# Grouped-query attention on one core: K transposed on VectorE in 32x32 blocks, scores in 32-row PE tiles, Q loaded plainly and replicated

## The chip, the cores and the metric

The kernel runs on one core of a Trainium2 chip. The metric is the device time of one execution in microseconds (us). The program uses five engines of the core, which run beside each other (in the kernel before PE, DVE and ACT were busy for 89%, 87% and 71% of the same 370.2 us) and wait for each other by semaphores: PE (matrix multiply), DVE (VectorE), ACT (ScalarE), POOL (GpSimd) and SP, which here only issues DMA. The order of each engine's instructions is fixed in the program. SBUF is the working memory that the program loads into, PSUM the memory that it lets PE write its results to.

Each run carries a state: "slow" if it is over 1.5% above the fastest run of the same kernel, "unknown" if the kernel ran only once, else "fast". Times below are medians of all runs; only e1, e2 and e6 have slow runs among them (one, two and two of four), and there the mean of the fast runs is given too. A ratio is the mean time of one kernel's fast runs over that of the other's fast runs of the same rounds, so it is not quite the ratio of the medians that are quoted.

## The reference

```python
B, Hq, Hkv, Sq, Sk, D = 16, 32, 8, 16, 2048, 128        # all bf16, values normal * 0.05
def reference(q, k, v):
    k = jnp.repeat(k, Hq // Hkv, axis=1); v = jnp.repeat(v, Hq // Hkv, axis=1)
    scores = jnp.einsum("bhqd,bhkd->bhqk", q, k) * D ** -0.5
    p = _softmax(scores, axis=-1)
    return jnp.einsum("bhqk,bhkd->bhqd", p, v)
```

Four query heads of 16 rows share one K and V, so there are 128 groups of 64 query rows. The kernel works on pairs of groups: 64 pairs, each with 128 query rows, two K and two V of 0.5 MB each.

## The kernel before

For a pair, PE transposes K in 128x128 pieces (32 of them) into a PSUM staging bank, DVE or ACT copies it to SBUF ("evacuation"), PE computes the scores S, DVE scales them and takes the row minimum of the negated scores, ACT takes the exponential P, PE transposes P, DVE or ACT evacuates it, PE computes P times V, and DVE or ACT normalises. Q arrives transposed: a transposing DMA does it.

```python
# SP: Q by transposing DMA, 16 of them, 512 rows each
sp.dma_start_transpose(QT[:, qch * c:qch * (c + 1)], qf[qch * c:qch * (c + 1), :]).then_inc(sem_q[c], 16)
...
# PE: K transposes into a staging bank, then scores
for t in range(8):
    j = 8 * h + t
    ins = pe.transpose(stage_ap(ld["bank"], t), Kn[s][:, j, :], ident[:, :])
...
for c in range(NCH):
    for gg in range(2):
        ins = pe.matmul(S_ps[64 * gg:64 * (gg + 1), 512 * c:512 * (c + 1)],
                        QT[:, 128 * p + 64 * gg:128 * p + 64 * (gg + 1)],
                        kt[:, gg, 4 * c:4 * (c + 1), :], start=True, stop=True)
```

The order of the instructions on each engine is fixed when the program is built: a planner walks through all operations with a table of assumed durations and an assumed hand-over latency, always takes the one that can start first, and chooses DVE or ACT for the operations that either can do.

Of the kernel before, what the change touches and what calls it, by code (L numbers as in the profile page):

```python
# [11 lines left out]
NBK = 12  # L12
NBV = 16
NBO = 8
NKT = 3
NPT = 3
NSTAGE = 3
DV = 3
DSTORE = 7
QCH = 512  # L20
QLEAD = 6
# [3 lines left out]
    "KT_load": 0.46, "PT_load": 0.46, "S": 0.75, "PV": 1.02,  # L25
    ("dve", "kte"): 0.63, ("dve", "pte"): 0.63, ("dve", "max"): 2.30, ("dve", "recip"): 0.17, ("dve", "norm"): 0.36,
    ("act", "kte"): 1.07, ("act", "pte"): 1.07, ("act", "exp"): 2.08, ("act", "norm"): 0.46,
    "K": 0.65, "V": 0.65, "ST": 0.65, "Q": 3.3,
}
_LAT = 0.12  # L30
_LAT_SAME = 0.04
_DMA_LAT = 2.0
_BW = 0.371
_BW_SLOW = 0.364
_RING_MB = 5.2
_SIZE = {"K": 0.5, "V": 0.5, "Q": 0.25 * 1.45, "ST": 0.03125 * 1.45}
_T0 = 7.0


def sp_program(NP, qch_pairs, dv=DV, dstore=DSTORE, qlead=QLEAD):  # L40
    sp = []
    n_qch = (NP + qch_pairs - 1) // qch_pairs
    q_step = {c: max(0, c * qch_pairs - qlead) for c in range(n_qch)}
    for t in range(NP + max(dv, dstore) + 1):
        if t < NP:
            sp += [("K", 2 * t), ("K", 2 * t + 1)]
        for c in range(n_qch):
            if q_step[c] == t:
                sp.append(("Q", c))
        if 0 <= t - dv < NP:  # L50
            sp += [("V", 2 * (t - dv)), ("V", 2 * (t - dv) + 1)]
        if 0 <= t - dstore < NP:
            sp.append(("ST", t - dstore))
    return sp


SCHED_OPTS = dict(kte_engs=("dve", "act"), pte_engs=("dve", "act"), norm_engs=("dve", "act"), eft=True)


def build_schedule(NP, qch_pairs, nbk=NBK, nbv=NBV, nbo=NBO, nkt=NKT, npt=NPT, nstage=NSTAGE, opts=None):  # L60
    INF = float("inf")
    DUR = _DUR
    opts = dict(SCHED_OPTS, **(opts or {}))
    sp = sp_program(NP, qch_pairs)
    done = {}

    def t(key):
        return done.get(key, INF)

    pe_left = []  # L70
    for p in range(NP):
        pe_left += [("KT", p, 0), ("KT", p, 1), ("S", p), ("PT", p), ("PV", p)]
    x_left = []
    for p in range(NP):
        x_left += [("kte", p, gg, h) for gg in range(2) for h in range(2)]
        x_left += [("pte", p, h) for h in range(2)]
        x_left += [("max", p), ("recip", p), ("exp", p), ("norm", p)]
    sp_left = list(sp)
    progs = {"pe": [], "dve": [], "act": [], "sp": []}
    free = {"pe": _T0, "dve": _T0, "act": _T0, "sp": _T0}  # L80
    load_u = {}
    next_u = [0]
    dma_fast_end = [0.0]
    dma_slow_end = [0.0]
    dma_hist = []
    issued_mb = [0.0]
    pe_sched = set()
    timeline = []

    def eng_options(op):  # L90
        k = op[0]
        if k in ("max", "recip"):
            return ("dve",)
        if k == "exp":
            return ("act",)
        if k == "kte":
            return opts["kte_engs"]
        if k == "pte":
            return opts["pte_engs"]
        return opts["norm_engs"]  # L100

    def ready_pe(op):
        kind = op[0]
        r = []
        if kind == "KT":
            p, gg = op[1], op[2]
            r.append(t(("dma", "K", 2 * p + gg)))
            if p >= nkt and ("S", p - nkt) not in pe_sched:
                return INF
            u0 = next_u[0]  # L110
            for h in range(2):
                if u0 + h >= nstage:
                    r.append(t(("evac", u0 + h - nstage)))
        elif kind == "S":
            p = op[1]
            r.append(t(("dma", "Q", p // qch_pairs)))
            for gg in range(2):
                for hh in range(2):
                    key = ("KT", p, gg, hh)
                    if key not in load_u:  # L120
                        return INF
                    r.append(t(("evac", load_u[key])))
            if p >= 1:
                r.append(t(("max", p - 1)))
        elif kind == "PT":
            p = op[1]
            r.append(t(("exp", p)))
            if p >= npt and ("PV", p - npt) not in pe_sched:
                return INF
            u0 = next_u[0]  # L130
            for h in range(2):
                if u0 + h >= nstage:
                    r.append(t(("evac", u0 + h - nstage)))
        elif kind == "PV":
            p = op[1]
            for hh in range(2):
                key = ("PT", p, None, hh)
                if key not in load_u:
                    return INF
                r.append(t(("evac", load_u[key])))  # L140
            for gg in range(2):
                r.append(t(("dma", "V", 2 * p + gg)))
            if p >= 1:
                r.append(t(("norm", p - 1)))
        return max(r) if r else 0.0

    def ready_x(op):
        kind = op[0]
        r = []
        if kind == "kte":  # L150
            key = ("KT", op[1], op[2], op[3])
            if key not in load_u:
                return INF
            r.append(t(("load", load_u[key])))
        elif kind == "pte":
            key = ("PT", op[1], None, op[2])
            if key not in load_u:
                return INF
            r.append(t(("load", load_u[key])))
        elif kind == "max":  # L160
            p = op[1]
            r.append(t(("S", p)))
            if p >= 2:
                r.append(t(("exp", p - 2)))
        elif kind == "recip":
            r.append(t(("exp", op[1])))
        elif kind == "exp":
            p = op[1]
            r.append(t(("max", p)))
            if p >= 2:  # L170
                r.append(t(("PT", p - 2)))
        elif kind == "norm":
            p = op[1]
            r += [t(("PV", p)), t(("recip", p))]
            if p >= nbo:
                r.append(t(("dma", "ST", p - nbo)))
        return max(r) if r else 0.0

    def ring_ok_time(size):
        need = issued_mb[0] + size - _RING_MB  # L180
        if need <= 0:
            return 0.0
        for tm, cum in dma_hist:
            if cum >= need:
                return tm
        return dma_hist[-1][0] if dma_hist else 0.0

    def ready_sp(op):
        kind, x = op
        r = [ring_ok_time(_SIZE[kind])]  # L190
        if kind == "K":
            if x >= nbk:
                r.append(t(("KT", (x - nbk) // 2, (x - nbk) % 2)))
        elif kind == "V":
            if x >= nbv:
                r.append(t(("PV", (x - nbv) // 2)))
        elif kind == "ST":
            r.append(t(("norm", x)))
        return max(r) if r else 0.0

    KIND_PRIO = {"S": 0, "max": 0, "exp": 0, "PT": 1, "pte": 1, "PV": 2, "recip": 2, "norm": 2, "KT": 3, "kte": 3}

    while pe_left or x_left or sp_left:
        best = None
        if sp_left:
            op = sp_left[0]
            rd = ready_sp(op)
            if rd < INF:
                st = max(free["sp"] + _LAT_SAME, rd + _LAT)
                best = ((round(st, 3), -1, -1), st, "sp", op)  # L210
        seen = 0
        for op in pe_left:
            rd = ready_pe(op)
            if rd == INF:
                continue
            st = max(free["pe"] + _LAT_SAME, rd + _LAT)
            cand = ((round(st, 3), op[1], KIND_PRIO[op[0]]), st, "pe", op)
            if best is None or cand[0] < best[0]:
                best = cand
            seen += 1  # L220
            if seen > 12:
                break
        seen = 0
        for op in x_left:
            rd = ready_x(op)
            if rd == INF:
                continue
            engs = eng_options(op)
            if opts["eft"] and len(engs) > 1:
                fin = [(max(free[e] + _LAT_SAME, rd + _LAT) + DUR[(e, op[0])], e) for e in engs]  # L230
                fin.sort()
                engs = (fin[0][1],)
            for eng in engs:
                st = max(free[eng] + _LAT_SAME, rd + _LAT)
                cand = ((round(st, 3), op[1], KIND_PRIO[op[0]]), st, eng, op)
                if best is None or cand[0] < best[0]:
                    best = cand
            seen += 1
            if seen > 24:
                break  # L240
# [401 lines left out]
```

## Time and profile before

| | before |
|---|---|
| time, median | 373.71 us (373.55 to 373.78, 3 runs) |
| span in the profile | 370.2 us |
| busy: PE, DVE, ACT | 331.0 (89%), 323.0 (87%), 261.9 (71%) us |
| HBM traffic | 134.2 MB read and 2.1 MB written, together 368 GB/s over the span |

From the profile's page: the busy times, and three rows of the table that cuts the span into 40 equal slices (about 9.3 us each). PEclk is the granted PE clock in tenths, DMA the busy share of the DMA engines in tenths, GB/s what they moved.

```profile
PE 331.0 (89%) x5632; PEld 260.2 (70%) x5632; DVE 323.0 (87%) x500; ACT 261.9 (71%) x269; POOL 1.0 (0%) x6
...
PEclk9899999999999999999999999999999999999999
DMA  7999999999999999999999999999999999999993
GB/s 262 375 408 341 408 352 405 405 345 407 352 407 410 342 408 350 406 409 347 410 347 408 400 350 413 348 410 370 380 410 346 408 350 399 409 410 410 406 410 112
```

The DMA row is at 9 nearly throughout. The GB/s row alternates between about 408 and about 345. The stretches table of the same run looks closer; its columns are the stretch, its length, busy time of each engine with the number of instructions, PE clock, DMA share, GB/s.

```profile
core 0: us, PE busy (x) PEld busy (x) DVE busy (x) ACT busy (x) POOL busy (x), PEclk, DMA share, GB/s
47.00:53.00 6.00, 5.42 (x96) 4.18 (x93) 5.40 (x10) 3.99 (x4) 0.00 (x0) 1.00 1.05 412
53.00:56.00 3.00, 3.00 (x68) 2.74 (x66) 3.00 (x5) 2.81 (x3) 0.00 (x0) 1.00 1.18 227
56.00:74.00 18.00, 16.16 (x276) 12.69 (x276) 15.84 (x25) 12.88 (x14) 0.00 (x0) 1.00 1.03 407
74.00:80.00 6.00, 5.78 (x99) 4.34 (x96) 5.51 (x9) 5.30 (x7) 0.00 (x0) 1.00 1.15 313
```

SP issues transposing Q loads at 43.3 and 66.3 us, and such a load lands 12.3 us after its issue in the median, so one is put into 53-56 us and one into 74-80 us. The DMA share is 1.18 and 1.15 there, and DMA moves much less (227 and 313 GB/s, against 412 and 407 in the other two stretches).

The groups of instructions that the change touches, from the page (busy us, mean ns of one, then the idle time in front of them and what ended most of it):

```profile
L575 DVE TENSOR_SCALAR_CACHE_REDUCE Sneg<-S_ps 128x2048 f32<-128x2048 f32 x64 | 146.7, 2292 | 18.6 <-PE S_ps L513 15.1
L501 PE MATMUL ST_ps<-ident,Kn 128*128 128x128 bf16 x2048 | 143.6, 223 | 18.6 <-ACT KT L595 8.1
...
L565 DVE COPY KT<-ST_ps 128x1024 bf16<-128x1024 bf16 x177 | 116.3, 683 | 9.8 <-PE ST_ps L501 7.6
...
L595 ACT ACTIVATE PT<-ST_ps 128x1024 bf16<-128x1024 bf16 x59 | 57.2, 1021 | 42.2 <-PE ST_ps L529 42.2
...
L513 PE MATMUL S_ps<-KT,QT 128*64 128x512 bf16 x512 | 68.4, 388 | 6.6 <-ACT KT L595 4.4
```

And one S with the P transposes after it in order of time on PE (start, length):

```profile
101.55 1.05 PE L513 MATMUL S_ps<-KT,QT 128*64 128x512 bf16 x8
102.53 1.07 PE L529 MATMUL ST_ps<-ident,P 128*128 128x128 bf16 x16
```

Eight matmuls of 128 rows take 1.05 us from first to last.

### The profile page before, as it was taken

Reading aid. Unit: us, or ns where it says so; the run is one execution under the profiler, and the core shown is the slowest. Engines: PE = TensorE matmul, PEld = TensorE weight load, DVE = VectorE, ACT = ScalarE, POOL = GpSimd, SP = SyncE. Lnnn points to the kernel's source line nnn. Section 1 sums busy time; section 2 is a strip of 40 time slices with the busy share of each in tenths; the row PEclk is TensorE's granted clock in tenths of the full one; section 3 lists DMA queues with packets and bytes.
Section 4 is the critical chain, followed back from the end, with each engine's and each line's share of the span. In section 5 each row is a group of like instructions: output and inputs, shape, how many; then the busy total and the mean of one; then the engine's idle time right before and its main releaser. Section 6 shows DMA issues by size and latency. Waiting matters only on the chain.

```text
span 370.2 us, 13021 instructions
## 1 busy us (share of the span) xinstructions
PE 331.0 (89%) x5632; PEld 260.2 (70%) x5632; DVE 323.0 (87%) x500; ACT 261.9 (71%) x269; POOL 1.0 (0%) x6
## 2 busy tenths in 40 slices
PE   4698998998998989999898999989999898999995
PEld 3576876776776767677776777777777676776764
DVE  2589998998998989899898998989899897999984
ACT  1267766895666885867878676795867778679593
POOL 1000000000000000000000000000000000000000
PEclk9899999999999999999999999999999999999999
DMA  7999999999999999999999999999999999999993
GB/s 262 375 408 341 408 352 405 405 345 407 352 407 410 342 408 350 406 409 347 410 347 408 400 350 413 348 410 370 380 410 346 408 350 399 409 410 410 406 410 112
DMA packets 54840, 139.26 MB, mean 376 GB/s; under 512 B 22016, under 2 KB 22016, under 8 KB 54784
## 3 DMA queue, kind: packets, MB, share of 16 engines
q1 hardware_dynamic: 54784, 138.43, 102.3%
q8 instruction: 45, 0.74, 0.8%
q14 instruction: 11, 0.09, 0.1%
HBM read 134.22 MB, written 2.10 MB: 368 GB/s over the span
## 4 chain that ended last, share of the span: by engine, by line
PE 68%; ACT 21%; issue 4%; DMA 4%; DVE 3%
PE ST_ps L501 26%; PE S_ps L513 17%; PE O_ps L544 14%; PE ST_ps L529 11%; ACT KT L595 11%; ACT PT L595 8%; DMA Vb<-in_v_dram 3%; DVE Sneg L575 2%; ACT P L601 1%; DMA Kn<-in_k_dram 1%; DVE KT L565 1%; DVE PT L565 0%; DVE O L586 0%; DVE rrec L569 0%
## 5 line engine op out<-in xcount | busy, mean ns | idle before, releaser
L575 DVE TENSOR_SCALAR_CACHE_REDUCE Sneg<-S_ps 128x2048 f32<-128x2048 f32 x64 | 146.7, 2292 | 18.6 <-PE S_ps L513 15.1
L501 PE MATMUL ST_ps<-ident,Kn 128*128 128x128 bf16 x2048 | 143.6, 223 | 18.6 <-ACT KT L595 8.1
L501 PEld LDWEIGHTS ST_ps<-ident,Kn 128*128 128x128 bf16 x2048 | 119.6, 99 | 45.1 <-issue 26.7
L601 ACT ACTIVATE P<-Sneg,nbias 128x2048 bf16<-128x2048 f32 x64 | 128.3, 2005 | 11.5 <-DVE Sneg L575 11.5
L565 DVE COPY KT<-ST_ps 128x1024 bf16<-128x1024 bf16 x177 | 116.3, 683 | 9.8 <-PE ST_ps L501 7.6
L595 ACT ACTIVATE KT<-ST_ps 128x1024 bf16<-128x1024 bf16 x79 | 77.6, 1022 | 48.4 <-PE ST_ps L501 48.3
L595 ACT ACTIVATE PT<-ST_ps 128x1024 bf16<-128x1024 bf16 x59 | 57.2, 1021 | 42.2 <-PE ST_ps L529 42.2
L529 PE MATMUL ST_ps<-ident,P 128*128 128x128 bf16 x1024 | 71.6, 220 | 7.5 <-ACT KT L595 3.8
L529 PEld LDWEIGHTS ST_ps<-ident,P 128*128 128x128 bf16 x1024 | 58.2, 98 | 25.1 <-issue 11.4
L513 PE MATMUL S_ps<-KT,QT 128*64 128x512 bf16 x512 | 68.4, 388 | 6.6 <-ACT KT L595 4.4
L544 PE MATMUL O_ps<-Vb,PT 128*64 128x128 bf16 x2048 | 69.6, 220 | 4.2 <-issue 1.4
L544 PEld LDWEIGHTS O_ps<-Vb,PT 128*64 128x64 bf16 x2048 | 59.1, 110 | 11.1 <-issue 2.5
L565 DVE COPY PT<-ST_ps 128x1024 bf16<-128x1024 bf16 x69 | 44.3, 683 | 3.4 <-PE ST_ps L529 3.2
L513 PEld LDWEIGHTS S_ps<-KT,QT 128*64 128x64 bf16 x512 | 25.3, 109 | 26.3 <-issue 9.9
L586 DVE TENSOR_SCALAR O<-O_ps,rrec 128x128 bf16<-128x128 f32 x62 | 21.5, 346 | 9.1 <-PE O_ps L544 9.1
L569 DVE RECIPROCAL rrec<-rowsum 128x1 f32<-128x1 f32 x64 | 10.2, 159 | 4.3 <-ACT P L601 4.1
L601 ACT ACTIVATION_READ_ACCUMULATOR P<-Sneg,nbias 128x1 f32 x64 | 12.9, 202 | 0.0
L575 DVE DVE_READ_ACCUMULATOR Sneg<-S_ps 128x1 f32 x64 | 5.3, 83 | 0.0
L601 ACT ACT_TABLE_LOAD x1 | 1.3, 1283 | 0.7 <-PEq L627 0.7
L612 ACT ACTIVATE O<-O_ps,rrec 128x128 bf16<-128x128 f32 x2 | 0.7, 368 | 0.4 <-PE O_ps L544 0.4
L433 POOL TENSOR_SCALAR ident<-iota_t 128x128 bf16<-128x128 int32 x1 | 0.5, 536 | 0.1
L431 POOL IOTA iota_t<- 128x128 int32 x1 | 0.2, 235 | 0.4 <-POOLq L627 0.4
(4 smaller groups left out, 0.4 us busy)
## 6 DMA issues: line engine op xcount, KB each, us to landing
Kn<-in_k_dram SPq DMA_DIRECT2D x128, 512.0 KB, 12.9
Vb<-in_v_dram SPq DMA_DIRECT2D x128, 512.0 KB, 12.9
out_dram<-O SPq DMA_DIRECT2D x64, 32.0 KB, 12.6
QT<-in_q_dram SPq DMA_TRANSPOSE x16, 12.3
```

The source lines that it names most:

```text
L433: gp.tensor_scalar(ident[:, :], iota_t[:, :], 0.0, None, op0=ALU.is_equal).then_inc(sem_id, 1)
L501: ins = pe.transpose(stage_ap(ld["bank"], t), Kn[s][:, j, :], ident[:, :])
L513: ins = pe.matmul(S_ps[64 * gg:64 * (gg + 1), 512 * c:512 * (c + 1)], QT[:, 128 * p + 64 * gg:128 * p + 64 * (gg + 1)], kt[:, gg, 4 * c:4 ...
L529: ins = pe.transpose(stage_ap(ld["bank"], t), P[p % 2][:, 128 * j:128 * (j + 1)], ident[:, :])
L544: ins = pe.matmul(O_ps[64 * gg:64 * (gg + 1), 0:128], pt[:, j, 64 * gg:64 * (gg + 1)], Vb[g % NBV][:, j, :], start=(j == 0), stop=(j == J ...
L565: dve.tensor_copy(evac_dst(ld), stage_bank_ap(ld["bank"])).then_inc(sem_ev["dve"], 1)
L569: dve.reciprocal(rrec[:, p:p + 1], rowsum[:, p:p + 1]).then_inc(sem_rec, 1)
L575: dve.tensor_scalar(Sneg[kk % 2][:, :], S_ps[:, :], -scale, None, op0=ALU.mult, op1=ALU.min, accum_out=nbias[:, kk:kk + 1],).then_inc(sem_ ...
L586: dve.tensor_scalar(Osb[s_][:, :], O_ps[:, 0:128], rrec[:, p:p + 1], None, op0=ALU.mult).then_inc(sem_nm["dve"], 1)
L595: act.activation(evac_dst(ld), stage_bank_ap(ld["bank"]), ACT.Copy).then_inc(sem_ev["act"], 1)
L601: act.activation(P[kk % 2][:, :], Sneg[kk % 2][:, :], ACT.Exp, bias=nbias[:, kk:kk + 1], scale=-1.0, accum_out=rowsum[:, kk:kk + 1],).then ...
L612: act.activation(Osb[s_][:, :], O_ps[:, 0:128], ACT.Copy, scale=rrec[:, p:p + 1]).then_inc(sem_nm["act"], 1)
```

## The change

The intent is to relieve PE, which is busy for 89% of the span, and to get rid of the transposing DMA. K is no longer transposed on PE. One DVE instruction per K (128x1024 words of 4 bytes, each a pair of bf16 values) takes its place, and the program reads its result as transposed in 32x32 blocks of words. That is not K transposed as a whole: each group of 32 partitions holds 32 words of the head dimension for its own keys. So each score is a sum of four matmuls that contract 32 rows each (two word blocks, two halves of a pair), and four row tiles of PE are meant to work beside each other, each on its own 512 columns of S_ps. Q must fit this layout: it is loaded plainly, replicated four times with a stride on POOL ("qr"), transposed on PE ("qt"), and evacuated by ACT ("qe"). The transposed Q of eight pairs (a "chunk") takes four such rounds, x = 0 to 3; they all go through one PSUM bank, QT_ps. The planner is rewritten too.

```diff
-NBK = 12                     # buffers for K
-NBV = 16                     # buffers for V
+NBK = 10
+NBV = 14
 ...
-DV = 3                       # pairs by which V loads lag behind K loads
 ...
-QCH = 512
-QLEAD = 6                    # pairs by which a Q load leads
+DV = 2
+QCH = 1024
+QLEAD = 5
 ...
 _DUR = { ...
+    "qt": 0.55, "S": 1.1, "pt": 0.54, "pv": 1.08,
+    ("dve", "kx"): 1.25, ... ("act", "pe"): 1.03, ("act", "qe"): 1.06, ... ("pool", "qr"): 1.6, ...
 _LAT = 0.12                  # assumed hand-over latency (as before)
 ...
+            if kind == "kx":
+                ins = eng.transpose(KT[(p // 2) % NKT][:, p % 2, :], Kn[p % NBK][:, :])      # int32 words
 ...
+                if kind == "qe":                                    # 1024 elements a partition
+                    dst = QT[p % 2][:, op[2], :].rearrange("d (a i) -> d i a", i=NI)         # NI = 8
+                    src = QT_ps[:, 0:qch].rearrange("d (i a) -> d i a", i=NI)
 ...
-                sp.dma_start_transpose(QT[:, qch * c:qch * (c + 1)], qf[qch * c:qch * (c + 1), :])
+                dst, src = Qn[s][:, :, :], qf[qch * x:qch * (x + 1), :].rearrange("(a i) d -> a i d", i=NI)
 ...
+                    for x in range(4):
+                        for a in range(4):
+                            for gg in range(2):
+                                kt = KT[p % NKT][32 * a:32 * (a + 1), gg, :].bitcast(BF16)
+                                kt = kt.rearrange("i (r b j e) -> i r b j e", b=2, j=32, e=2)
+                                ins = pe.matmul(
+                                    S_ps[64 * gg:64 * (gg + 1), 512 * a:512 * (a + 1)],
+                                    QT[c % 2][32 * a:32 * (a + 1), x, 128 * pp + 64 * gg:128 * pp + 64 * (gg + 1)],
+                                    kt[:, :, x // 2, :, x % 2],
+                                    start=(x == 0), stop=(x == 3), tile_position=(32 * a, 64 * gg))
```

The Q load puts eight consecutive query rows into one partition, so after the transpose the columns stand in the order (i, a), and the evacuation puts them back to (a, i).

## The prediction

> **What bounds the kernel now.** The DMA engines. The page's 40-slice table shows their busy share at nine tenths or more from the second slice to the last but one, and the queue table books 102% of the span. Most slices move 405 to 413 GB/s; about every third falls to 341-352. There are 16 transposing Q loads (one per four pairs, about 23 us), spaced like the dips. The table of stretches: 400-411 GB/s around, but 227 in 53-56 us, and 341 and 285 in 74-80 us. Against 410 that is about 0.55 MB, or 1.4 us, lost per Q load: 16 x 1.4 = 22 us. Check: 139.3 MB at 408 GB/s is 341 us; plus 22, plus about 1.5 head and 6 tail, is 370.5; the span is 370.2. PE (331 us busy, 89%) and DVE (323, 87%) come next. The chain of waits names PE for 68%, but PE follows the loads.
>
> **What the change does.**
> - Removes the 16 transposing loads. Q arrives plainly, in 2 KB runs, same bytes. The load floor becomes about 341 us.
> - PE loses 2048 K transposes (about 1.96 us a pair by the chain's pieces), keeps P transposes (1.05) and PV (1.05). S turns from 8 matmuls (1.05 us) into 32 with 32 rows each, eight tiles at a time. [...] With Q transposes (0.3) PE needs about 3.6 us a pair, 230 us in all.
> - K evacuations vanish: 177 on DVE (116 us) and 79 on ACT (78 us). Instead DVE does 128 transposes of 128x1024 words. [...] scaled from the 2048-element reduction (2.29 us) that is an estimated 1.2 us each, 155-160 us.
> - P evacuations go mostly to ACT (1.02 us each). ACT gains 32 Q evacuations (about 34 us). Pool replicates Q, hidden.
>
> Totals, estimated: DVE 64 x (2 x 1.24 + 2.37 + 0.16) = 321, plus a few evacuations, about 327 us. ACT: exp 141 + P up to 130 + Q 34 + norm 24 = about 327. PE 230. DMA 341.
>
> **Critical path.** Loads stay the limit; the gain is the 22 us of Q transposes. DVE and ACT sit at 95% of the load time, so their own start (first scores at about 12 us) and tail matter: 327 plus about 15 is also near 342-345. S(p) waits for the reduction of p-1, but two K transposes (2.5 us) cover it. Span about 349-350, plus the 3.5 us by which time exceeds span before, plus 1 for stalls where the limits meet: **354 us**, range **348 to 365**. Faster by over 2%: 0.88; within 2%: 0.06; slower: 0.06.
>
> **What would show each step right.** No dips in the DMA row, 400-412 GB/s in nearly every slice; K transposes at 1.2-1.3 us; S about 1.1-1.4 us from first to last matmul; PE near 60-65%; DVE and ACT each above 90%.
>
> **What would make it wrong.** (a) Row tiles don't overlap, or the 4-byte stride of the moving operand slows them: above 2.5 us per S the DVE cover breaks, above 3 us PE becomes the limit. (b) The word transpose runs at half rate: DVE would need 480 us. (c) Pool's copies take much longer than planned, and the fixed order stalls PE and ACT at every Q chunk: some us each. (d) DVE and ACT, both nearly full, miss each other's results, and DMA shows gaps: up to 10 us. (e) Fewer K and V buffers starve the queue.

PE's sum came to about 3.6 us a pair: P transposes 1.05, PV 1.05, Q transposes 0.3 and about 1.2 for the scores; 64 times that is the 230 us. The 1.2 us of a K transpose stays as an estimate from the measured reduction (2.29 us for 2048 elements); that a transposed word costs as much as a reduced element was not shown at that time. Both were measured after it: 1.08 us for the scores of a pair and 1.225 us for a K transpose, below.

## The result, and the profile after

| | before | after |
|---|---|---|
| time, median | 373.63 us (373.02 to 373.78, 4 runs) | 477.17 us (473.6 to 479.55, 4 runs) |
| ratio of the fast runs | | 1.278 (95%: 1.271 to 1.285) |
| span in the profile | 370.2 us | 473.1 us |
| busy: PE, DVE, ACT | 331, 323, 262 us | 276, 327, 381 us |
| mean granted PE clock | 0.995 | 0.825 |

The change made the kernel 28% slower. The same rows of the page, after:

```profile
PE 275.6 (58%) x5376; PEld 194.3 (41%) x5376; DVE 327.2 (69%) x369; ACT 381.1 (81%) x308; POOL 28.9 (6%) x34
...
PEclk9999877975898677966899667995579776779999
DMA  8951978995889549995599839998299972999990
GB/s 300 413 220 49 348 265 286 360 413 182 308 315 401 197 169 407 352 361 182 213 406 400 319 133 332 340 408 306 89 353 320 401 278 115 340 337 363 411 367 10
```

DVE's work came out as forecast (about 327 us). PE was busy for 275.6 us where 230 was forecast, part of it at a lowered clock, and ACT for 381.1 us where about 327 was forecast. DMA is no longer saturated: its rate falls to 49 GB/s in the fourth slice and to 89, 115 and 133 in others. The clock row shows PE losing its full clock again and again, down to 5 tenths. The groups of the page:

```profile
L251 DVE TENSOR_SCALAR_CACHE_REDUCE Sneg<-S_ps 128x2048 f32<-128x2048 f32 x64 | 146.5, 2289 | 66.2 <-PE S_ps L327 64.1
L274 ACT ACTIVATE QT<-QT_ps 128x1024 bf16<-128x1024 bf16 x32 | 151.1, 4723 | 13.5 <-PE QT_ps L315 13.4
L244 DVE STREAM_TRANSPOSE KT<-Kn 128x1024 int32<-128x1024 int32 x128 | 153.5, 1225 | 2.4 <-DMA Kn<-in_k_dram 2.3
...
L274 ACT ACTIVATE PT<-PT_ps 128x1024 bf16<-128x1024 bf16 x92 | 94.9, 1072 | 31.2 <-PE PT_ps L337 31.2
...
L327 PE MATMUL S_ps<-KT,QT 32*64 32x512 bf16 x2048 | 89.5, 469 | 21.3 <-DVE KT L244 13.7
...
L249 POOL COPY Qr<-Qn 128x1024 bf16<-128x1024 bf16 x28 | 28.0, 1040 | 347.9 <-DMA Qn<-in_q_dram 346.7
```

The K transpose takes 1225 ns, as forecast; two of them in a row took 2.37 us (from 194.90 us), where one reduction of 2048 elements takes 2.29 us. The Q evacuation on ACT, which reads PSUM in order and writes SBUF with a step of eight bf16, that is 16 bytes, takes **4723 ns**, while the P evacuation, with the same 128x1024 bf16 from PSUM to SBUF, takes 1072 ns. 32 of them take 151.1 us of ACT; at the 1.06 us of the planner's table it would have been 34. What this does to the flow of work is seen in the timeline of ACT (start, length, instruction) in one Q pass of the changed kernel, the P evacuations and normalisations left out:

```profile
199.70 2.00 ACT L254 ACTIVATE P<-Sneg,nbias 128x2048 bf16<-128x2048 f32 x1
...
201.94 4.73 ACT L274 ACTIVATE QT<-QT_ps 128x1024 bf16<-128x1024 bf16 x1
...
207.86 4.72 ACT L274 ACTIVATE QT<-QT_ps 128x1024 bf16<-128x1024 bf16 x1 [0.34 <-PE QT_ps L315]
...
213.78 4.72 ACT L274 ACTIVATE QT<-QT_ps 128x1024 bf16<-128x1024 bf16 x1 [1.09 <-PE QT_ps L315]
217.99 2.21 ACT L254 ACTIVATE P<-Sneg,nbias 128x2048 bf16<-128x2048 f32 x1
...
220.18 4.74 ACT L274 ACTIVATE QT<-QT_ps 128x1024 bf16<-128x1024 bf16 x1
```

Between the exponentials at 199.70 and 217.99 us lie three Q evacuations, and after the second exponential comes a fourth. In this stretch there is one exponential in 18 us; outside a Q pass the trace has one in about 4.7 us. Who waits for whom (us in total, times, longest):

```profile
DVE Sneg L251 <- PE S_ps L327: 64.1, 14, 15.6
PE QT_ps L315 <- ACT QT L274: 56.7, 18, 4.9
```

PE waits for the single Q bank to be emptied before it can transpose the next round. Its next instruction in line may be a score, which then waits too, and DVE waits for that score. The longest of DVE's waits, 15.6 us, is the start of the kernel: the four slow evacuations of the first chunk stand in front of the first scores, which begin at 28.1 us (in e2, below, at 13.6 us; the prediction had about 12).

The new scores as such are as fast as the old ones. PE's timeline after, the scores of two pairs (32 matmuls of 32 rows each):

```profile
201.43 1.08 PE L327 MATMUL S_ps<-KT,QT 32*64 32x512 bf16 x32
...
213.67 1.93 PE L327 MATMUL S_ps<-KT,QT 32*64 32x512 bf16 x32
```

The first took 1.08 us, at full clock (1.00 from 201.43 to 202.51 us), against 1.05 us for the eight matmuls before. One matmul of either kind lasts about as long (median 375 ns in e2, below, and 379 ns before), so the 32 would have taken an estimated 4 x 1.05 = 4.2 us at the pace of the old ones: the row tiles do overlap, an estimated 4.2 / 1.08 = 3.9 times. The second lies in the Q pass, after PE had stood idle (for 3.05 us until 212.73 us); the granted clock from 213.7 to 215.6 us was 0.50, and it took 1.93 us.

### The profile page after: what moved, and what is told of

It is laid out like the page before. It is cut to its first block, busy times and chain, and to the rows that moved or that the text cites. A ratio compares the mean times of both kernels' runs of the same rounds, so it can differ in the third digit from the quotient of the medians.

```text
span 473.1 us, 11999 instructions
## 1 busy us (share of the span) xinstructions
PE 275.6 (58%) x5376; PEld 194.3 (41%) x5376; DVE 327.2 (69%) x369; ACT 381.1 (81%) x308; POOL 28.9 (6%) x34
## 4 chain that ended last, share of the span: by engine, by line
issue 16%; ACT 14%; PE 12%; DVE 4%; DMA 3%; POOL 1%; SPq 1%; ACTq 0%; POOLq 0%
ACT PT L274 7%; ACT QT L274 5%; PE S_ps L327 4%; PE O_ps L342 4%; PE PT_ps L337 3%; DMA Qn<-in_q_dram 3%; ACT P L254 2%; DVE Sneg L251 1%; DVE PT L274 1%; POOL Qr L249 1%; DVE KT L244 1%; PE QT_ps L315 1%; SPq L301 1%; ACTq L277 0%; ACT O L263 0%
## 5 line engine op out<-in xcount | busy, mean ns | idle before, releaser
L274 ACT ACTIVATE QT<-QT_ps 128x1024 bf16<-128x1024 bf16 x32 | 151.1, 4723 | 13.5 <-PE QT_ps L315 13.4
L244 DVE STREAM_TRANSPOSE KT<-Kn 128x1024 int32<-128x1024 int32 x128 | 153.5, 1225 | 2.4 <-DMA Kn<-in_k_dram 2.3
L274 ACT ACTIVATE PT<-PT_ps 128x1024 bf16<-128x1024 bf16 x92 | 94.9, 1072 | 31.2 <-PE PT_ps L337 31.2
L327 PE MATMUL S_ps<-KT,QT 32*64 32x512 bf16 x2048 | 89.5, 469 | 21.3 <-DVE KT L244 13.7
L337 PE MATMUL PT_ps<-ident,P 128*128 128x128 bf16 x1024 | 84.4, 248 | 11.8 <-ACT P L254 11.6
L337 PEld LDWEIGHTS PT_ps<-ident,P 128*128 128x128 bf16 x1024 | 72.2, 113 | 40.5 <-ACT P L254 29.0
L315 PE MATMUL QT_ps<-ident,Qr 128*128 128x128 bf16 x256 | 27.0, 270 | 84.6 <-ACT QT L274 56.7
L327 PEld LDWEIGHTS S_ps<-KT,QT 32*64 32x64 bf16 x2048 | 30.7, 120 | 49.8 <-issue 20.7
L249 POOL COPY Qr<-Qn 128x1024 bf16<-128x1024 bf16 x28 | 28.0, 1040 | 347.9 <-DMA Qn<-in_q_dram 346.7
L274 DVE COPY PT<-PT_ps 128x1024 bf16<-128x1024 bf16 x36 | 24.1, 689 | 32.1 <-PE PT_ps L337 32.0
```

What stands on the lines that cost most here:

```text
L244: ins = eng.transpose(KT[(p // 2) % NKT][:, p % 2, :], Kn[p % NBK][:, :])
L249: ins = eng.activation(dst, src, ACT.Copy) if me == "act" else eng.tensor_copy(dst, src)
L274: ins = eng.activation(dst, src, ACT.Copy) if me == "act" else eng.tensor_copy(dst, src)
L315: ins = pe.transpose(QT_ps[:, 128 * i:128 * (i + 1)], Qr[:, x, i, :], ident[:, :],)
L327: ins = pe.matmul(S_ps[64 * gg:64 * (gg + 1), 512 * a:512 * (a + 1)], QT[c % 2][32 * a:32 * (a + 1), x, 128 * pp + 64 * gg:128 * pp + 64 * ...
L337: ins = pe.transpose(PT_ps[h][:, 128 * t:128 * (t + 1)], P[p % 2][:, 128 * r:128 * (r + 1)], ident[:, :])
```

## The experiments

Twelve kernels ran. The kernel before ran beside them; its medians were 372.7 to 373.8 us. The theories:

- **A**: the loss is the price of the Q evacuation, and the price comes from the 16-byte step of its write.
- **A-order**: the price matters only because the fixed order was planned for 1.06 us.
- **B**: the new kernel is slow for other reasons as well (32-row tiles, an order that is too tight, the halved clock).
- **C** and **D** are two accounts of what is left after e1; the expectations of e6 to e8 say what they are.
- and, for the kernel before: whether the transposing loads really cost 22 us of the time.

All twelve results passed the comparison with the reference, including three (e4, e6, e9) that compute with a wrong or permuted Q. That comparison says little about Q here: with inputs of 0.05 the scores are so small that the softmax is nearly flat. That is argued from the inputs; for e1, e2 and the kernels built on them it was checked on paper that every element of Q lands where the changed kernel puts it.

### e1: the permutation on the read side

```diff
-                    dst = QT[p % 2][:, op[2], :].rearrange("d (a i) -> d i a", i=NI)
-                    src = QT_ps[:, 0:qch].rearrange("d (i a) -> d i a", i=NI)
+                    dst = QT[p % 2][:, op[2], :].rearrange("d (a i) -> d a i", i=NI)
+                    src = QT_ps[:, 0:qch].rearrange("d (i a) -> d a i", i=NI)
```

> Same order of instructions as after; only the Q evacuation changes: it writes its 1024 elements in order and does the permutation on the read side (from PSUM, 256 bytes between neighbours) instead of writing with 16 bytes between neighbours. Theory A (the price of the 16-byte-step write into SBUF, 4.72 us x 32 against about 1.05, is the whole loss): one Q evacuation takes 1.0 to 1.2 us, the total falls to 350-362 us, the granted clock returns to above 0.97. Theory A2 (any permutation costs ScalarE that much, on either side): still about 4.7 us each and 470-480 us. Theory B (the new kernel is slow for other reasons too, 32-row tiles, a fixed order with two engines near full): evacuations get short but the total stays above 380 us.

Measured: 372.79 us (368.88 to 375.36, 4 runs), ratio to before 0.995 (0.988 to 1.002). The mean of the three fast runs is 371.5 us. The group of the Q evacuations:

```profile
L274 ACT ACTIVATE QT<-QT_ps 128x1024 bf16<-128x1024 bf16 x32 | 32.6, 1019 | 13.8 <-PE QT_ps L315 13.8
```

One evacuation took 1.02 us. The order on all engines was the same as in the changed kernel, so these two lines are worth 104 us (477.2 to 372.8). A is confirmed for the bulk, A2 is out. But 350-362 us was not reached, and the clock stayed at 0.92. The total fell neither where A put it nor above 380 where B put it: something else is left, 17 to 19 us above the forecast of 354. It is called the residual below. (The profiled run of e1 counts as slow; for other lines of this order e2 is shown.)

### e2: the permutation in the load

```diff
-        ... qf[qch * x:qch * (x + 1), :].rearrange("(a i) d -> a i d", i=NI)      # runs of 2 KB
+        ... qf[qch * x:qch * (x + 1), :].rearrange("(i a) d -> a i d", i=NI)      # runs of 256 B
-                    dst = QT[p % 2][:, op[2], :].rearrange("d (a i) -> d i a", i=NI)
+                    dst = QT[p % 2][:, op[2], :].rearrange("d (i a) -> d i a", i=NI)
```

> Same order as after; Q is loaded in the permuted order (256-byte runs instead of 2 KB), so that the evacuation is a plain copy on both sides. Theory A and A2: evacuation 1.02-1.06 us like the P evacuations, total 350-362 us; the 256-byte runs of 2.1 MB cost at most a few us of DMA. Theory B: above 380 us.

Measured: 375.44 us (371.28 to 377.81, 4 runs), ratio 0.998 (0.992 to 1.004). The two fast runs have a mean of 372.6 us. The instructions on the transposed Q (min, median and max duration in ns):

```profile
L274 ACT ACTIVATE QT<-QT_ps x32: 1002/1020/1023, 5.9 to 299.2; 128x1024 bf16<-128x1024 bf16 x32
```

A contiguous write costs the same 1.02 us as the read with a step in e1. And the total is again at the level of before, not below 362 us.

### e5: the same evacuation in four ways

Of the four evacuations of a Q pass, x = 0 is done by ACT with the step on the write, x = 1 by ACT with the step on the read, x = 2 by DVE with the step on the write, x = 3 by DVE with the step on the read.

```diff
+                    if x == 0:   ins = eng.activation(wd, ws, ACT.Copy)      # L276: write step 16 bytes
+                    elif x == 1: ins = eng.activation(rd, rs, ACT.Copy)      # L278: read step 256 bytes
+                    elif x == 2: ins = eng.tensor_copy(wd, ws)               # L280: write step 16 bytes
+                    else:        ins = eng.tensor_copy(rd, rs)               # L282: read step 256 bytes
```

> Prices the Q evacuation itself: of the four evacuations of a Q pass one is done by ScalarE with the 16-byte-step write, one by ScalarE with the step on the PSUM read side, one by VectorE with the 16-byte-step write, one by VectorE with the step on the read side. If the step of the write is dear only on ScalarE: 4.7, 1.0, about 1.1-1.2, about 1.1-1.2 us. If the SBUF write is dear for any engine: VectorE with the step write also 3 us or more. The total is not the point (one slow evacuation a pass instead of four, so about 375-410 us).

Measured: one look, 423.63 us. The four groups of this run:

```profile
L276 ACT ACTIVATE QT<-QT_ps 128x1024 bf16<-128x1024 bf16 x8 | 37.7, 4718 | 1.1 <-PE QT_ps L328 1.1
L280 DVE COPY QT<-QT_ps 128x1024 bf16<-128x1024 bf16 x8 | 37.6, 4701 | 3.0 <-PE QT_ps L328 3.0
...
L282 DVE COPY QT<-QT_ps 128x1024 bf16<-128x1024 bf16 x8 | 9.7, 1216 | 0.1
...
L278 ACT ACTIVATE QT<-QT_ps 128x1024 bf16<-128x1024 bf16 x8 | 8.2, 1022 | 2.2 <-PE QT_ps L328 2.2
```

The write step costs 4.70 us on DVE and 4.72 us on ACT. Two engines pay the same, so the price does not belong to ScalarE but to writing SBUF in this pattern. Of the two expectations, the one that only ScalarE pays fell, and the other (DVE also 3 us or more) held. The read step is free for ACT (1.02 us, as in e1 and as for the plain copy of e2); DVE takes 1.22 us with it, where it takes 0.68 us for a contiguous P evacuation. The total lies above the expected 375-410 us, which had counted one slow evacuation a pass; there are two, and the order was planned for 1.06 us. It was not followed up.

### e9: other write steps

The four evacuations on ACT with destination steps of 2, 4, 16 and 64 bf16 (4, 8, 32 and 128 bytes) and a contiguous read. Q ends up permuted. Built on e8.

```diff
+                    w = lambda n: QT[p % 2][:, x, :].rearrange("d (a i) -> d i a", i=n)
+                    if x == 0:   ins = eng.activation(w(2), r(2), ACT.Copy)      # L272: 4 bytes
+                    elif x == 1: ins = eng.activation(w(4), r(4), ACT.Copy)      # L274: 8 bytes
+                    elif x == 2: ins = eng.activation(w(16), r(16), ACT.Copy)    # L276: 32 bytes
+                    else:        ins = eng.activation(w(64), r(64), ACT.Copy)    # L278: 128 bytes
```

> Prices the ScalarE write step: in the four evacuations of a Q pass the destination steps are 4, 8, 32 and 128 bytes (2, 4, 16 and 64 elements), the source in PSUM is read in order, 1024 elements each; Q ends up permuted, wrong on purpose. [...] 4 and 8 bytes about 1.0 us, 32 and 128 bytes as dear as 16 bytes, 4.7 us or more. Rival (any write that is not contiguous is dear, or the cost grows with the step): 4 and 8 bytes already 2 us or more, or 32 and 128 bytes clearly above 4.7. The total is not the point.

Measured: one look, 415.26 us. The four groups:

```profile
L278 ACT ACTIVATE QT<-QT_ps 128x1024 bf16<-128x1024 bf16 x8 | 38.1, 4764 | 1.3 <-PE QT_ps L324 1.2
L276 ACT ACTIVATE QT<-QT_ps 128x1024 bf16<-128x1024 bf16 x8 | 36.1, 4510 | 1.1 <-PE QT_ps L324 1.1
...
L274 ACT ACTIVATE QT<-QT_ps 128x1024 bf16<-128x1024 bf16 x8 | 19.7, 2460 | 2.4 <-PE QT_ps L324 2.4
...
L272 ACT ACTIVATE QT<-QT_ps 128x1024 bf16<-128x1024 bf16 x8 | 10.5, 1311 | 3.7 <-PE QT_ps L324 3.3 <-PE S_ps L336 0.2
```

| write step | 2 bytes (e2) | 4 | 8 | 16 (after) | 32 | 128 |
|---|---|---|---|---|---|---|
| us for 1024 elements | 1.02 | 1.31 | 2.46 | 4.72 | 4.51 | 4.76 |

From 4 to 16 bytes the price nearly doubles with each doubling of the step (1.31, 2.46, 4.72), and then it stays within 6%. The first three lie near a straight line: between 4 and 8 bytes the price grows by (2.46 - 1.31) us / 4 = 0.29 us per byte of step, between 8 and 16 by (4.72 - 2.46) us / 8 = 0.28 us, and some 0.2 us come on top (an estimate from these three figures). The steps of 32 and 128 bytes leave the line: there it is 4.51 and 4.76 us, that is 4.4 to 4.7 ns an element, where the contiguous write takes 1.02 us, 1.0 ns an element. Why the price grows up to a step of 16 bytes and no further, no run shows. Of the expectation's first set one half fell (about 1.0 us at 4 and 8 bytes: it was 1.31 and 2.46, the latter 2.4 times the contiguous write), and the other held (32 and 128 bytes as dear as 16: within 5% of 4.72). The rival (2 us or more at 4 and 8 bytes already) came true for 8 bytes only.

### e3: the planner knows the price

```diff
-    ... ("act", "qe"): 1.06 ...
+    ... ("act", "qe"): 4.72 ...
```

> The slow write stays, but the planner is told 4.72 us instead of 1.06 for it, so the fixed order on every engine is built around it and more P evacuations go to VectorE. Theory A-time (the engine time itself, 117 us more on ScalarE): ScalarE and VectorE together then need about 327+327+117 us, so the two balance near 385-395 and the total cannot fall below about 395; I expect 400-430. Theory A-order (most of the loss is the order that was built for 1.06 us, everything queued behind it): the total falls to below 395. If the loss is in neither, it stays at 470-480.

Measured: 423.64 us (419.95 to 425.93), ratio 1.137 (1.131 to 1.142). Knowing the price saves 54 us of the 477: the planner moved P evacuations from ACT to DVE (79 on DVE instead of 36). The other half of the loss stays, as A-time expected (400-430). So a wrong entry in the planner's table made the loss larger, but a right one does not cure it.

### e11: another order, the slow write kept

The changed kernel with the planner constants of e8 (below), nothing else.

> The changed kernel with nothing but the new planner constants; the 16-byte-step write stays. It tells whether order alone could have cured the change. If the write's engine time rules (32 x 3.7 us = 118 us more, through one Q bank): still 440-475 us. If the new order hides it: below 400 us.

Measured: 461.68 us (457.64 to 462.75), ratio 1.236 (1.230 to 1.241). The same order without the slow write is e10, 356.5 us. So the slow write is worth 105 us in this order and was worth 104 in the other. That is a little less than the engine time it takes: by the evacuations themselves 151.1 - 32.6 = 118.5 us, by ACT's busy time 381.1 - 268.1 (e1) = 113 us. The expectation that another order could hide it (below 400 us) fell.

### e4: the kernel before with plain Q loads

```diff
-                sp.dma_start_transpose(QT[:, qch * c:qch * (c + 1)], qf[qch * c:qch * (c + 1), :]).then_inc(sem_q[c], 16)
+                sp.dma_start(QT[:, qch * c:qch * (c + 1)], qf[qch * c:qch * (c + 1), :].rearrange("(a i) d -> a (i d)", i=qch // 128)).then_inc(sem_q[c], 16)
```

> The kernel before with its 16 transposing Q loads replaced by plain loads of the same bytes in 1 KB runs; the result is wrong on purpose (Q is not transposed). Theory of the prediction (the transposing loads take 22 us of the DMA engines): span 348-352, time 350-356 us, no dips in the DMA row. Rival (PE or VectorE bound, the dips only coincide): 368-374 us, unchanged.

Measured: 367.84 us (367.29 to 368.83), ratio 0.986 (0.982 to 0.989). Q is not transposed. From its page: the two DMA rows, and the chain of waits by engine:

```profile
DMA  7999999999999999999999999999999999999620
GB/s 289 414 408 406 411 403 411 411 409 409 408 412 409 411 410 407 411 410 409 412 407 409 409 395 406 404 394 409 402 404 385 409 398 398 389 396 407 230 101 14
...
PE 70%; ACT 22%; issue 3%; DVE 3%; DMA 1%
```

The dips are gone and the loads finish about two slices early, but the time falls by 5.5 us only. Summed along the two GB/s rows, the first 120 MB have arrived after about 316 us before and after about 298 us here. So the transposing loads cost the DMA about 19 us, somewhat less than the 22 of the prediction. The kernel before had a second limit just behind: the chain through PE and the evacuations, at some 366 us. The prediction called the kernel DMA-bound; it was bound by both.

### e6: one Q pass only

Built on e2. The copies, transposes and evacuations of all chunks but the first are dropped; the scores all use the first chunk's Q (wrong). Q loads and the order of the rest stay.

```diff
+    late = lambda op: op[0] in ("qr", "qt", "qe") and op[1] > 0
+    progs = {e: [op for op in prog if not late(op)] for e, prog in progs.items()}
...
-                                    QT[c % 2][32 * a:32 * (a + 1), x, ...
+                                    QT[0][32 * a:32 * (a + 1), x, ...
```

> The kernel with the permuted load, with the Q copies, Q transposes and Q evacuations of all chunks but the first left out (all scores use the first chunk's Q, wrong on purpose; the Q loads stay; the order of everything else is unchanged). The permuted-load kernel took 375.4 us where 354 was predicted. Theory C (the residual is the Q pass, its work and the way the fixed order places it): 353-360 us, and the clock above 0.97. Theory D (the residual is the cold PE clock, or an order that is too tight everywhere): above 365 us.

Measured: 367.07 us (361.24 to 368.89; two of four runs slow), ratio 0.972 (0.964 to 0.980), where e2 had 0.998. The Q passes' work accounts for some 8 to 10 us of the residual, not for all of it. The median lies in D's range (above 365 us), but of the fast runs one (361.2 us) lies between C and D and the other (365.4 us) at D's edge. The run is inconclusive between C and D.

### e7: PE kept warm

Built on e2; five dummy transposes into the idle Q bank ahead of PE's waits.

```diff
 ...
+                elif waits.seen.get(sem_eng["act"].name, 0) >= last_qe:
+                    for _ in range(5):
+                        pe.transpose(QT_ps[:, 0:128], ident[:, :], ident[:, :])
```

> The permuted-load kernel with five dummy 128x128 transposes ahead of PE's waits (for scores, P transposes and PV, into the Q bank when it is idle), so that PE stays busy in its gaps. Theory D (the residual is the half clock that PE falls to in its gaps, S and PV then take 1.9 us instead of 1.08): granted clock above 0.98 and a gain of 8 us or more, 362-367 us. Theory C (the order of the Q pass): clock rises but the total moves by less than 3 us or gets worse.

Measured: 376.11 us (375.41 to 376.79), ratio 1.006 (1.002 to 1.011). The granted clock rose from 0.921 to 0.986, and the time did not fall. So keeping PE warm in this way gains nothing. It does not show that the halved clock costs nothing: the dummies also take PE time (283.8 us busy instead of 245.0), and in the page's chain of work that ended last they hold 9% of the span themselves. What they cost may hide what the clock gave.

### e8: another fixed order

Built on e2. The same instructions, three constants of the planner. They were found by replaying many orders on paper with durations measured in these runs.

```diff
-DV = 2
+DV = 3
-QLEAD = 5
+QLEAD = 8
-_LAT = 0.12
+_LAT = 0.16
```

> The permuted-load kernel with another fixed order, from three constants of the planner alone: assumed hand-over latency 0.16 instead of 0.12 us, Q loaded eight pairs ahead instead of five, V three pairs behind K instead of two. Same instructions otherwise. Theory C (the order loses the residual): 350-360 us, DMA row without gaps at 405-412 GB/s until near the end. Theory D (work or clock, not order): 368-378 us as before.

Measured: 359.91 us (359.44 to 360.45), ratio 0.963 (0.959 to 0.966). That is 15.5 us below e2 by the medians and 12.7 by the fast runs, with the same operations: most of the residual lies in what the planner decides. That is more than the order. The new plan also moves 20 P evacuations from DVE to ACT (16 on DVE instead of 36), so DVE is busy for 311.7 us instead of 325.5 and ACT for 284.5 instead of 268.2. Order and division of work changed together, and no run separates them. What is different shows in what ended PE's idle time ahead of the instructions on the transposed K, the scores. In e2 (us, times):

```profile
  DVE KT L244: 41.5, 35
...
  DVE Sneg L251: 5.7, 2
```

The scores of e2 wait 41.5 us for a K transpose that DVE has not yet done; what stood in front of it was not followed up. In the best kernel (e10, next; e8 has 75.6 and 3.1 us) the K transposes are done ahead, and the scores wait for the reduction of the pair before, which frees the score bank:

```profile
  DVE Sneg L251: 72.4, 68
...
  DVE KT L244: 1.6, 3
```

### e10: the order of e8 with the read step of e1

```diff
 (the changed kernel, with the two lines of e1 and the three constants of e8)
```

> The order with the new constants together with the step on the PSUM read side, so that Q is loaded in 2 KB runs again. The permuted 256-byte loads left small dips in the DMA row (365-384 GB/s in the slices with a Q load). Expect 355-359 us, that is 1 to 4 us below the 359.9 us of the permuted-load kernel with the new order, DMA row without those dips; if the run length of the Q loads doesn't matter, 359-361 us.

Measured, five rounds: 356.47 us (355.84 to 357.16, 5 runs), ratio to before 0.956 (0.954 to 0.958). It beats both kernels: 4.4% below before and a quarter below the changed kernel. Its page:

```profile
PE 234.1 (66%) x5376; PEld 167.5 (47%) x5376; DVE 312.2 (88%) x352; ACT 284.6 (80%) x325; POOL 29.0 (8%) x34
...
DMA  7999999999999999999999999999999999999981
GB/s 286 415 408 356 411 411 407 411 412 408 412 414 410 407 409 415 409 409 410 400 399 409 409 409 411 409 410 414 406 406 410 405 400 413 410 408 413 401 313 38
```

DMA moves 399 to 415 GB/s in every slice from the second to the last but two, except the fourth (356). In e2 the same row reads

```profile
GB/s 272 391 409 409 411 408 385 412 410 411 398 380 411 377 395 362 405 372 289 413 375 404 411 411 398 365 412 370 406 350 369 405 311 375 394 387 413 410 266 9
```

with many slices below 400 from the eleventh on. And PE in e10 waits for loads:

```profile
PE O_ps L342 <- DMA Vb<-in_v_dram: 23.6, 18, 3.1
```

e2 has no such entry: there PE never waited for V. The gain over e8 is 3.4 us by the medians and about 2.5 by the ratios, in the expected range. The order is the same and an evacuation takes 1.03 us in both, so it is put down to the 2 KB runs of the Q loads in place of 256-byte runs; e8's GB/s row dips to 365-386 in seven slices between the fourth and the thirty-third, and e10's only once.

### e12: one constant of the three

Built on e1, with the assumed hand-over latency alone at 0.16.

> The read-stride kernel (372.8 us) with one planner constant changed, the assumed hand-over latency 0.16 instead of 0.12 us; Q lead and V lag stay at 5 and 2. It splits the 16 us between that kernel and the best one. If the order of the compute engines (K transposes planned ahead of the P evacuations, fewer P evacuations on VectorE) is what was gained: 357-364 us, and PE's waits for K transposes fall well below the 41 us of the read-stride kernel. If it was the load order (Q eight pairs ahead, V three pairs behind): 369-374 us.

Measured: 362.36 us (360.44 to 365.24), ratio 0.972 (0.967 to 0.978). The order of the loads is the same as in e1, so 10 of the 16 us between e1 and e10 (9 of 15 by the fast runs) come with the changed plan of the compute engines alone (29 P evacuations on DVE instead of 36, and scores waiting 28.9 us for K transposes instead of 41.5 in e2). The other 6 come when the load constants change too, and these change the compute engines' plan once more (16 P evacuations on DVE in e10). The 0.16 us were not chosen for being truer than 0.12; the planner takes what can start first, and a small shift tips many of its choices. Why these choices are better was not taken further.

## Why the prediction was wrong

The prediction said 354 us (348 to 365), and the changed kernel took 477.

1. **The step that failed: "ACT gains 32 Q evacuations (about 34 us)".** They measured 151 us. This term of the sum was mis-sized by a factor of 4.5, and with the write cured 104 of the 123 us of the miss are gone. In their place the runs showed ACT and the one Q bank holding up the Q pass: one exponential in 18 us in place of one in 4.7. The number had come from the planner's table (1.06) and from the P evacuation, which moves as many elements in 1.02 us; the access pattern of the destination was not looked at. The diff shows a write step of 16 bytes, and no run had yet priced a copy with such a step. e1, e2, e5 and e9 show the cause, e11 its size, 105 us.
2. The list of what could go wrong did not have it. It suspected the row tiles, the word transpose and POOL's copies, and all three behaved: S at 1.08 us at full clock (forecast 1.1-1.4; 1.93 at half clock), the K transpose at 1.225 us (1.2-1.3), POOL's copies at 1.04 us.
3. **"Loads stay the limit"** failed too, in the second place. With the write cured and the order unchanged, time was 372.8 us. The engines' fixed plan (their order, and which of them does a P evacuation), not DMA, was the limit; item (d) had put up to 10 us on such misses, and another plan gained 16. It could have been asked before the run: build_schedule in kernel.py, called with 64 pairs and 8 pairs a chunk, returns the end that the planner itself expects, and that is 381 us for the changed kernel even at 1.06 us a Q evacuation (375 for e12's plan, 368 for e10's; measured without the slow write 373, 362 and 356). With e10's plan DMA moves 399 GB/s or more in nearly every slice and PE waits for V, so loads are close to the limit again, and the time is 356.5 us. That this is only 2.5 us above the forecast is luck in part: it is another plan than the one forecast, its span (354.3 us) is 4 to 5 us above the forecast's, and the 3.5 us that the forecast added between span and time are about 1.8 in every profiled run here (356.12 - 354.3 in e10).
4. "The gain is the 22 us of Q transposes": DMA did lose about 19 us to them, but e4 shows that removing them alone brings 5.5 us, since PE and the evacuations were a second limit close behind. On this reading the 16 us of e10 come from relieving both.
5. DVE was forecast at about 327 us busy and was at 327; PE at 230 and was at 276, of which part is the halved clock (in e10 234). "DVE and ACT each above 90%" did not come about in any of the good versions (88% and 80% in e10).

Not settled: what single order constraint makes e1's order slow, how much of e8's gain is the order and how much the 20 P evacuations that DVE no longer does, how much the halved clock costs by itself, whether a second Q bank would have hidden part of the slow write (none was tried), and why the price of the write grows up to a step of 16 bytes (4.72 us) and no further.

## What to carry to other kernels

Price a copy by its destination pattern, not by its element count: on the way into SBUF write in order (here a step of 4 bytes already cost 1.3 times the contiguous write, one of 16 bytes 4.6 times), and put a needed permutation on the PSUM read of an ACT copy, where it was free here (1.02 us with a read step of 256 bytes in e1 and without one in e2). An engine time that is off in a planner's table is lost twice, once as time and once as order; measure each instruction form once before planning with it. Before calling a kernel bound by one thing, ask how far behind the next limit is, and try the removal alone: here about 19 us of freed DMA time brought 5.5.
